# Decode attention with a 268 MB cache: p.v with the values moving in four column groups, keys folded in place, wo as four rows a lane

## The chip, the cores and the metric

The kernel runs on one core of one Trainium2 chip. The metric is the device time of one execution in microseconds; several runs are taken and their median is given. The profile comes from one profiled execution. Engines are named as the profile names them: PE is TensorE (PEld its weight loads), DVE VectorE, ACT ScalarE, POOL GpSimd, SP SyncE. Nearly all transfers are issued on SP's queue and are carried by the core's 16 DMA engines.

## The reference

The output is the input plus an attention block and a gated MLP block, both on the normalised input. There is one new token for each of four batch entries, and every one of the 32 heads has its own cache of 4096 keys and values of 128 bf16 numbers.

```python
# x: (4, 1, 640); k_cache, v_cache: (4, 32, 4096, 128); wq: (640, 4096); wo: (4096, 640)
q = (xn @ wq) as (4, 32, 1, 128)
scores = einsum('bhqd,bhkd->bhqk', q, k) * 128 ** -0.5
p = softmax(scores)
o = einsum('bhqk,bhkd->bhqd', p, v)
attention = o as (4, 1, 4096) @ wo
# gMLP: z = gelu(xn @ w_in); z1, z2 = halves of z (864 each); g = w_sp * layernorm(z2) + b_sp
result = x + attention + (z1 * g) @ w_out
```

Keys and values are 134 MB each and are read once. A key meets a single query, so the scores are a matrix times a vector for each pair of batch entry and head.

## The kernel before

**Tiles and slots.** Four heads of one batch entry make a tile: 128 partitions ("lanes"), 32 lanes a head, and in each lane 128 rows (NC) of 128 numbers, 4 MB. There are 32 tiles of keys and 32 of values (NT = 32; tile i belongs to head group i // 4 and batch entry i % 4). A pool of five slots (`kv`) holds them. The first three slots hold wq (two loads) and the gMLP's weights at the start. `load` (L115) fetches one tile in one transfer on SP; the last tile of values comes in four pieces, 64, 32, 16 and 16 rows of a lane (`V_CUTS`). `pump` (L137) issues loads in a fixed order, roughly v(i), k(i+2), as far as the tile that held the slot has been marked as used; the transfer itself waits on the engines that last touched the slot. At two places (`EXTRA_K`) two key tiles follow each other, so that at the end the keys are ahead and the last four tiles to come are values. `load_wo` (L148) fetches the 640 KB of wo that one head group needs, in the third of its four tiles; the last one comes as four pieces of 160 KB, behind everything else.

**Scores of a tile.** `stage_q` (L365) brings the query into every lane: four matmuls spread the four heads' queries over 32 lanes each (four groups of 32 columns of PE), and ACT copies the result to bf16. The scores come in four quarters: `product` (L381) multiplies a quarter of the keys with the query on DVE into a buffer `prod`; `fold_half` (L390) adds the upper 64 of the 128 products to the lower 64 into `folded`. After each half, `sums` (L402) lets PE add these 64 numbers down to 8: eight matmuls with the identity, each over 512 columns, into one PSUM bank. `row_sums` (L415) reduces the 8 to one on DVE. The second half's `row_sums` of a tile stands in the next tile's step.

**Softmax.** `lane_max` (L425) takes the largest score of each lane, `turn_max` (L430) turns these 128 numbers into one row by an fp32 transpose on PE, `head_max` (L435) takes the maximum of each head, `spread_max` (L446) spreads the negative scaled maxima over all lanes by an fp32 matmul, and `exps` (L453) computes the exponentials on ACT, head by head, with their sums per lane into `acc`. The weights go to `p_m`: for each of the 128 rows of a lane four columns, one a head, with zeros where a lane belongs to another head.

**p.v.** `weighted` (L469) makes the values the stationary operand: for each of the 128 rows of a lane it loads 128x128 values as weights and moves four columns of `p_m` through; the result, 128 numbers of the head dimension on partitions by head and batch entry, gathers in PSUM. After the fourth tile of a group, `group_den` (L485) sums `acc` over the lanes by an fp32 matmul with ones and inverts it on DVE, `group_norm` (L494) scales, and `group_proj` (L501) multiplies by wo into `out_ps`.

**Order.** The order on PE, DVE, ACT and SP is written out by hand in the loop at L536. The p.v of tile i - 1 (later i - 2 and i - 3) stands in step i, behind the first `sums`. Each step ends with marking the keys as used and with `pump`. Behind the loop (L571 to L591) come the last tile's softmax, the p.v of the last two tiles of values, the last projection and the output. At the start, q is projected by 160 matmuls with wq as the stationary operand (L216), and the gMLP runs ahead of the loop.

Of the kernel before, what the change touches and what calls it, by code (L numbers as in the profile page):

```python
# [16 lines left out]
EXTRA_K = (24, 28)  # L17


@with_exitstack  # L20
def kernel(
# [31 lines left out]
    NQ = 4  # L53
    QC = NC // NQ
# [7 lines left out]
    NOH = D // 2  # L62

    const = ctx.enter_context(tc.tile_pool(name="const", bufs=1))
    kv = ctx.enter_context(tc.tile_pool(name="kv", bufs=KV_SLOTS))
    wop = ctx.enter_context(tc.tile_pool(name="wop", bufs=1))
    prod = ctx.enter_context(tc.tile_pool(name="prod", bufs=1))
    fold = ctx.enter_context(tc.tile_pool(name="fold", bufs=2))
# [5 lines left out]
    ps_m = ctx.enter_context(tc.tile_pool(name="ps_m", bufs=2, space=PSUM))  # L74
# [4 lines left out]


# [64 lines left out]
    wo_v = A_wo.rearrange("(j h p) n -> j p h n", p=P, h=HT)  # L145
    wo_tiles = {}

    def load_wo(j):  # L148
        wo_tiles[j] = wop.tile([P, HT, D], BF16, name="wo")
        if j == HG - 1:  # L150
            for hh in range(HT):
                nc.sync.dma_start(out=wo_tiles[j][:, hh, :], in_=wo_v[j][:, hh, :])
            return
        nc.sync.dma_start(out=wo_tiles[j][:], in_=wo_v[j])
# [3 lines left out]


    ident = const.tile([P, P], BF16)  # L160
    make_identity(nc, ident[:])
    ident_f = const.tile([P, P], FP32)
    nc.vector.tensor_copy(out=ident_f[:], in_=ident[:])
# [4 lines left out]
    scale_row = const.tile([1, P], FP32)  # L168
    nc.vector.memset(scale_row[:], scale_qk)
# [4 lines left out]
    p_m = [const.tile([P, NC, HT], BF16, name=f"pm{b}") for b in range(Bsz)]  # L174
    acc = [const.tile([P, HT, Bsz], FP32, name=f"acc{g}") for g in range(NACC)]
    for t in p_m + acc:
        nc.gpsimd.memset(t[:], 0.0)


# [29 lines left out]
    xnT = const.tile([P, DC, Bsz], BF16)  # L209
    nc.vector.tensor_copy(out=xnT[:], in_=xnT_ps[:])  # L210

    q_ps = ps_m.tile([P, H, Bsz], FP32, tag="m", name="q_ps")
    for h in range(H):
        for c in range(DC):
            t, i = wq_parts[c]
            nc.tensor.matmul(  # L216
                out=q_ps[:, h, :],
                lhsT=t[:, i, h * Dh : (h + 1) * Dh],
                rhs=xnT[:, c, :],
                start=(c == 0),  # L220
                stop=(c == DC - 1),
            )
    qT = const.tile([P, H, Bsz], BF16)
    nc.vector.tensor_copy(out=qT[:], in_=q_ps[:])  # L224


# [15 lines left out]


# [10 lines left out]
    def gmlp():  # L254
        zz, gw, gt, gz, sq = (gm[n] for n in ("zz", "gw", "gt", "gz", "sq"))
        zT = ps_pv.tile([P, 2, NFC, Bsz], FP32, tag="pv", name="zT")
        for t in range(2):
            f1 = t * Fh + NFF * P
            w_t = w_in_sb[:, :, t * Fh : f1].rearrange("p c (f k) -> p c k f", k=NFF)
            for k in range(NFC):  # L260
                for c in range(DC):
                    nc.tensor.matmul(
                        out=zT[: P if k < NFF else FT, t, k, :],
                        lhsT=w_t[:, c, k, :] if k < NFF else w_in_sb[:, c, f1 : f1 + FT],
                        rhs=xnT[:, c, :],
                        start=(c == 0),
                        stop=(c == DC - 1),
                    )
# [94 lines left out]
    folds, sums_ps, maxes = {}, {}, {}  # L363

    def stage_q(i):  # L365
        hg, b = divmod(i, Bsz)
        qb_ps = ps_m.tile([P, Dh], FP32, tag="m", name="qbc_ps")
        for hh in range(HT):
            nc.tensor.matmul(  # L369
                out=qb_ps[hh * LN : (hh + 1) * LN, :],  # L370
                lhsT=qT[:, HT * hg + hh, b : b + 1].to_broadcast([P, LN]),
                rhs=ident[:],
                start=True,
                stop=True,
            )
        qbcs[i] = small.tile([P, Dh], BF16, name="qbc", bufs=3)
        nc.scalar.copy(out=qbcs[i][:], in_=qb_ps[:])  # L377

    prods = {}

    def product(i, q):  # L381
        t = prods[i, q] = prod.tile([P, QC, Dh], BF16, name="prod")
        nc.vector.tensor_tensor(  # L383
            out=t[:],
            in0=k_tiles[i][:, q * QC : (q + 1) * QC, :],
            in1=qbcs[i][:, None, :].to_broadcast([P, QC, Dh]),
# [3 lines left out]
    def fold_half(i, q):  # L390
        t = prods.pop((i, q))
        half, part = divmod(q, 2)
        if part == 0:
            folds[i, half] = fold.tile([P, HC, HD2], BF16, name="folded")
        nc.vector.tensor_tensor(  # L395
            out=folds[i, half][:, part * QC : (part + 1) * QC, :],
            in0=t[:, :, 0:HD2],
            in1=t[:, :, HD2:Dh],
            op=ALU.add,
        )  # L400

    def sums(i, half):  # L402
        t = folds.pop((i, half))
# [21 lines left out]
    def lane_max(i):  # L425
        m1 = small.tile([P, 1], FP32, name="m1")
        nc.vector.tensor_reduce(out=m1[:], in_=scores[i][:], axis=AX.X, op=ALU.max)  # L427
        maxes[i] = m1

    def turn_max(i):  # L430
        mT = ps_m.tile([1, P], FP32, tag="m", name="mT")
        nc.tensor.transpose(out=mT[:], in_=maxes[i][:], identity=ident_f[:])  # L432
        maxes[i] = mT

    def head_max(i):  # L435
        nm = small.tile([1, HT], FP32, name="nm")
        nc.vector.tensor_reduce(  # L437
            out=nm[:],
            in_=maxes[i][:].rearrange("a (h p) -> a h p", h=HT),
            axis=AX.X,  # L440
            op=ALU.max,
            negate=True,
        )
        maxes[i] = nm

    def spread_max(i):  # L446
        nb_ps = ps_m.tile([P, HT], FP32, tag="m", name="nb_ps")
        nc.tensor.matmul(  # L448
            out=nb_ps[:], lhsT=scale_row[:], rhs=maxes[i][:], start=True, stop=True
        )  # L450
        maxes[i] = nb_ps

    def exps(i):  # L453
        hg, b = divmod(i, Bsz)
        nb = small.tile([P, HT], FP32, name="nb")
        nc.scalar.copy(out=nb[:], in_=maxes.pop(i)[:])  # L456
        s_sb, pm, a = scores.pop(i), p_m[b], acc[hg % NACC]
        for hh in range(HT):
            ps = slice(hh * LN, (hh + 1) * LN)
            nc.scalar.activation(  # L460
                out=pm[ps, :, hh],
                in_=s_sb[ps, :],
                func=ACT.Exp,
                bias=nb[ps, hh : hh + 1],
# [4 lines left out]
    def weighted(i, c0=0, c1=NC):  # L469
        hg, b = divmod(i, Bsz)  # L470
        if b == 0 and c0 == 0:
            pvs[hg] = ps_pv.tile([P, HT, Bsz], FP32, tag="pv", name="pv")
        v_nat, pm = v_tiles[i], p_m[b]
        for c in range(c0, c1):
            nc.tensor.matmul(  # L475
                out=pvs[hg][:, :, b],
                lhsT=v_nat[:, c, :],
                rhs=pm[:, c, :],
                start=(c == 0),
                stop=(c == NC - 1),  # L480
            )

    gr = {}

    def group_den(hg):  # L485
        den = ps_m.tile([P, HT, Bsz], FP32, tag="m", name="den")
        nc.tensor.matmul(  # L487
            out=den[:], lhsT=ones_sq[:], rhs=acc[hg % NACC][:], start=True, stop=True
        )
        rden = small.tile([P, HT, Bsz], FP32, name="rden")  # L490
# [3 lines left out]
    def group_norm(hg):  # L494
        o_n = small.tile([P, HT, Bsz], BF16, name="o_n")
        nc.vector.tensor_tensor(
            out=o_n[:], in0=pvs.pop(hg)[:], in1=gr[hg][:], op=ALU.mult
        )
        gr[hg] = o_n
# [20 lines left out]

    turns = {}
# [8 lines left out]
    with tc.manual_schedule(engines={E.PE, E.DVE, E.Activation, E.SP}):  # L530
# [5 lines left out]
        for i in range(NT):  # L536
            j = turns.get(i)
            product(i, 0)
            fold_half(i, 0)
            at(i - 1, row_sums, 1)  # L540
            at(i - 1, lane_max)
            at(i - 1, turn_max)
            group(turns.get(i - 1, -1), group_proj)
            product(i, 1)
            at(i - 1, head_max)
            at(i - 1, spread_max)
            at(i - 1, exps)
            fold_half(i, 1)
            sums(i, 0)
            product(i, 2)  # L550
            if i + 2 < NT:
                stage_q(i + 2)
            fold_half(i, 2)
# [3 lines left out]
            for jj in due:  # L557
                weighted(jj)
                group(jj, group_den)
# [62 lines left out]
```

## Time and profile before

| what | value |
|---|---|
| median of three runs | 673.95 us (673.77 to 673.96) |
| span of the profiled execution, first to last instruction | 671.3 us |
| runs' median over that span (what lies around it) | 2.65 us |
| mean granted TensorE clock | 0.627 |
| busy: DVE, PE, ACT | 507.1, 392.5, 94.4 us |
| bytes moved, mean rate | 282.98 MB, 422 GB/s |

The page does not give the profiled execution's own time, only its span; the difference to the median of the runs is taken as what lies around it. The span is cut into 40 slices for the rows of busy tenths, where 9 stands for 90% or more. A group row gives a line of the kernel, the engine, the operation, output and inputs, shapes and count; then busy time, mean duration in ns, and the idle time in front with what ended it. A row of the windows view gives start and end, the length, busy time and number of instructions on PE, PEld, DVE, ACT and POOL, and at the end the granted clock, the mean busy share of the 16 DMA engines and GB/s. In a DMA queue row stand packets, MB and the time of the packets as a share of 16 engines' span; the queue called "instruction" brings the programs of the engines.

### The profile page before, as it was taken

To read this page: it belongs to the slowest core of one execution; us is meant where nothing else is said; L and a number is where in the kernel's file an instruction comes from. 1 tells how busy PE (TensorE), PEld (TensorE's weight loads), DVE (VectorE), ACT (ScalarE), POOL (GpSimd) and SP (SyncE) were. 2 spreads that over 40 slices of the span, in tenths; PEclk is the share of its full clock that TensorE was granted. 3 is DMA by queue.
4 is the path that set the end of the run, shared out by engine and by line. 5 is a ranking of instruction groups with operands and counts; after the bars stand their busy time and mean duration, and the time that the engine had idled before them with its cause. 6 is when DMAs were issued, how large, how long until landed. Compare 5 with 4: busy or idle time off the path is not lost.

```text
span 671.3 us, 11493 instructions
## 1 busy us (share of the span) xinstructions
PE 392.5 (58%) x5193; PEld 213.8 (32%) x5193; DVE 507.1 (76%) x433; ACT 94.4 (14%) x329; POOL 2.7 (0%) x13
## 2 busy tenths in 40 slices
PE   1627765546656456574556755456655557556576
PEld 1503333233333233342233333133333224233154
DVE  1299896966779777787777788676786999876961
ACT  0202111101111101111101111101111111101111
POOL 1000000000000000000000000000000000000000
PEclk9999675666656556666575556566666655656566
DMA  9999999999999999999999999999999999999995
GB/s 371 418 437 436 429 426 428 429 425 432 430 426 431 431 427 431 427 428 430 431 431 421 433 430 427 429 425 429 430 436 423 429 435 430 418 432 429 433 418 203
DMA packets 14684, 282.98 MB, mean 422 GB/s; under 512 B 1344, under 2 KB 5548, under 8 KB 5932
## 3 DMA queue, kind: packets, MB, share of 16 engines
q1 hardware_dynamic: 14616, 282.25, 98.5%
q8 instruction: 40, 0.66, 0.4%
q14 instruction: 8, 0.07, 0.0%
q10 hardware_dynamic: 20, 0.01, 0.0%
HBM read 282.24 MB, written 0.01 MB: 420 GB/s over the span
## 4 chain that ended last, share of the span: by engine, by line
DMA 55%; DVE 27%; PE 16%; issue 1%; SPq 0%; DVEq 0%
DMA k_nat<-in_A_k_cache_dram 50%; DVE prod L383 15%; PE s_ps L407 8%; DVE folded L395 8%; PE pv L475 7%; DMA v_nat<-in_A_v_cache_dram 6%; DVE s_sb L418 3%; DVE m L427 1%; DVE nm L437 0%; PE den L487 0%; PE qbc_ps L369 0%; DVE rden L491 0%; PE out_ps L505 0%; SPq L100 0%; SPq L89 0%
## 5 line engine op out<-in xcount | busy, mean ns | idle before, releaser
L383 DVE TENSOR_TENSOR prod<-k_nat,qbc 128x4096 bf16<-128x4096 bf16 x128 | 292.7, 2287 | 82.8 <-DMA k_nat<-in_A_k_cache_dram 81.2
L407 PE MATMUL s_ps<-folded,ident 128*128 128x512 bf16 x512 | 225.5, 619 | 80.8 <-DVE folded L395 80.4
L395 DVE TENSOR_TENSOR folded<-prod 128x2048 bf16<-128x2048 bf16 x128 | 156.1, 1220 | 3.3
L407 PEld LDWEIGHTS <-ident 128*128 128x128 bf16 x512 | 71.1, 139 | 190.7 <-issue 189.9
L475 PE MATMUL pv<-pm,v_nat 128*128 128x4 bf16 x4096 | 111.3, 167 | 3.5 <-issue 3.0
L475 PEld LDWEIGHTS <-v_nat 128*128 128x128 bf16 x4096 | 108.9, 100 | 7.1 <-issue 3.7
L432 PE MATMUL mT<-ident_f,m 128*1 128x128 f32 x32 | 11.2, 350 | 111.7 <-DVE m L427 111.7
L460 ACT ACTIVATE pm<-s_sb,nb 32x128 bf16<-32x128 f32 x128 | 74.0, 578 | 2.6
L456 ACT COPY nb<-nb_ps 128x4 f32<-128x4 f32 x32 | 5.2, 162 | 475.8 <-PE nb_ps L448 475.8
L448 PE MATMUL nb_ps<-nm,scale_row 1*128 1x4 f32 x64 | 17.7, 345 | 59.0 <-DVE nm L437 59.0
L418 DVE TENSOR_REDUCE s_sb<-s_ps 128x64 f32<-128x512 f32 x64 | 43.6, 682 | 9.6 <-PE s_ps L407 6.5
L432 PEld LDWEIGHTS mT<-ident_f,m 128*1 128x1 f32 x32 | 2.5, 79 | 138.5 <-DVE m L427 102.3
L448 PEld LDWEIGHTS nb_ps<-nm,scale_row 1*128 1x128 f32 x64 | 15.6, 302 | 68.6 <-issue 57.2
L460 ACT ACTIVATION_READ_ACCUMULATOR pm<-s_sb,nb 32x1 f32 x128 | 32.2, 251 | 0.0
L491 DVE RECIPROCAL rden<-den 128x16 f32<-128x16 f32 x8 | 2.1, 258 | 32.6 <-PE den L487 32.6
L377 ACT CAST qbc<-qbc_ps 128x128 bf16<-128x128 f32 x32 | 8.4, 266 | 78.5 <-PE qbc_ps L369 78.4
L369 PEld LDWEIGHTS <-qT 128*32 128x32 bf16 x128 | 3.4, 99 | 24.3 <-issue 23.8
L224 DVE CAST qT<-q_ps 128x128 bf16<-128x128 f32 x1 | 0.3, 291 | 14.3 <-PE q_ps L216 14.3
L216 PE MATMUL q_ps<-xnT,wq 128*128 128x4 bf16 x160 | 4.6, 167 | 9.5 <-DMA wq<-in_A_wq_dram 9.5
L427 DVE TENSOR_REDUCE m<-s_sb 128x1 f32<-128x128 f32 x32 | 9.2, 286 | 1.1
L437 DVE TENSOR_REDUCE nm<-mT 1x4 f32<-1x128 f32 x32 | 8.7, 272 | 0.5 <-PE mT L432 0.5
L369 PE MATMUL qbc_ps<-ident,qT 128*32 128x128 bf16 x128 | 8.8, 272 | 0.4 <-DVE qT L224 0.4
(69 smaller groups left out, 54.1 us busy)
## 6 DMA issues: line engine op xcount, KB each, us to landing
k_nat<-in_A_k_cache_dram SPq DMA_DIRECT2D x32, 4096.0 KB, 43.6
v_nat<-in_A_v_cache_dram SPq DMA_DIRECT2D x31, 4096.0 KB, 35.6
wo<-in_A_wo_dram SPq DMA_DIRECT2D x7, 640.0 KB, 44.5
wq<-in_A_wq_dram SPq DMA_DIRECT2D x1, 4096.0 KB, 12.2
w_sb<-in_B_w_in_dram SPq DMA_DIRECT2D x1, 2160.0 KB, 19.0
v_nat<-in_A_v_cache_dram SPq DMA_DIRECT2D x1, 2048.0 KB
wq<-in_A_wq_dram SPq DMA_DIRECT2D x1, 1024.0 KB, 14.2
v_nat<-in_A_v_cache_dram SPq DMA_DIRECT2D x1, 1024.0 KB
```

Of the source, the lines that this page charges most:

```text
L369: nc.tensor.matmul(out=qb_ps[hh * LN : (hh + 1) * LN, :], lhsT=qT[:, HT * hg + hh, b : b + 1].to_broadcast([P, LN]), rhs=ident[:], start=True,
L377: nc.scalar.copy(out=qbcs[i][:], in_=qb_ps[:])
L383: nc.vector.tensor_tensor(out=t[:], in0=k_tiles[i][:, q * QC : (q + 1) * QC, :], in1=qbcs[i][:, None, :].to_broadcast([P, QC, Dh]), op=ALU ...
L395: nc.vector.tensor_tensor(out=folds[i, half][:, part * QC : (part + 1) * QC, :], in0=t[:, :, 0:HD2], in1=t[:, :, HD2:Dh], op=ALU.add,)
L407: nc.tensor.matmul(out=s[:], lhsT=ident[:], rhs=t[:, :, g * RW : (g + 1) * RW], start=(g == 0), stop=(g == n - 1),)
L418: nc.vector.tensor_reduce(out=scores[i][:, half * HC : (half + 1) * HC], in_=sums_ps.pop((i, half))[:], axis=AX.X, op=ALU.add,)
L427: nc.vector.tensor_reduce(out=m1[:], in_=scores[i][:], axis=AX.X, op=ALU.max)
L432: nc.tensor.transpose(out=mT[:], in_=maxes[i][:], identity=ident_f[:])
L437: nc.vector.tensor_reduce(out=nm[:], in_=maxes[i][:].rearrange("a (h p) -> a h p", h=HT), axis=AX.X, op=ALU.max, negate=True,)
L448: nc.tensor.matmul(out=nb_ps[:], lhsT=scale_row[:], rhs=maxes[i][:], start=True, stop=True)
L460: nc.scalar.activation(out=pm[ps, :, hh], in_=s_sb[ps, :], func=ACT.Exp, bias=nb[ps, hh : hh + 1], scale=scale_qk, accum_out=a[ps, hh, b : ...
L475: nc.tensor.matmul(out=pvs[hg][:, :, b], lhsT=v_nat[:, c, :], rhs=pm[:, c, :], start=(c == 0), stop=(c == NC - 1),)
```

## The change

The change rewrites several steps.

- The projection of q swaps its operands: the normalised input, widened from 4 to 32 columns, is the stationary operand, and wq moves through in pieces of 512 columns, four groups of 32 PE columns side by side. The rows that come out (`q_rows`) are spread over the lanes by one matmul a tile with one column of the identity (`stage_q`), and ACT copies the four heads' parts in four copies.
- The keys are multiplied in place, half a tile at a call, and folded in place. `prod` and `folded` are gone, and PE's `sums` read the key slot itself, with 128 numbers from row to row instead of 64.
- The maximum over the lanes of a head is taken on DVE by a transpose in blocks of 32x32 and a second reduce. The fp32 transpose and the spreading matmul on PE are gone.
- p.v swaps its operands too: 32 columns of `p_m` (two batch entries x four rows of a lane x four heads, half of them zero) are the stationary operand and 512 values of a lane move through. 32 such matmuls a tile go round four column groups, two tiles gather in one PSUM bank, and each row is multiplied with the values of all four positions. ACT copies the bank to SBUF (`take`), and `group_pick` selects the matching blocks by eight fp32 matmuls with a mask (`pick`). `group_turn` scales by the denominators and transposes in blocks of 32x32, which leaves the head dimension as p = 4 rows a lane; wo is therefore loaded as four consecutive rows a lane (5120 bytes in a run where 1280 were).
- The last group ends in its own way: the first half of the last tile goes by the column groups and the selection, the rest by 64 matmuls with the values stationary as before, and wo comes by head as before.
- wo has two buffers, the small PSUM pool three banks instead of two.

The diff, cut to its core:

```diff
+    wop = ctx.enter_context(tc.tile_pool(name="wop", bufs=WO_BUFS))
...
-        nc.sync.dma_start(out=wo_tiles[j][:], in_=wo_v[j])
+        nc.sync.dma_start(out=wo_tiles[j][:], in_=rows.rearrange("(p j) n -> p j n", j=HT))
...
+                nc.tensor.matmul(
+                    out=q_ps[g * QD : (g + 1) * QD, :],
+                    lhsT=xnT[:, c, :],
+                    rhs=t[:, i, hg * GW : (hg + 1) * GW],
+                    start=(c == 0),
+                    stop=(c == DC - 1),
+                )
...
+        for hh in range(HT):
+            ps = slice(hh * LN, (hh + 1) * LN)
+            nc.scalar.copy(out=qbcs[i][ps, :], in_=qb_ps[ps, hh, :])
+
+    def product(i, half):
         nc.vector.tensor_tensor(
+            out=half_of(i, half),
+            in0=half_of(i, half),
+            in1=qbcs[i][:, None, :].to_broadcast([P, HC, Dh]),
             op=ALU.mult,
         )
...
+            out=t[:, :, 0:HD2], in0=t[:, :, 0:HD2], in1=t[:, :, HD2:Dh], op=ALU.add
...
+    def head_max(i):
         m1 = small.tile([P, 1], FP32, name="m1")
         nc.vector.tensor_reduce(out=m1[:], in_=scores[i][:], axis=AX.X, op=ALU.max)
+        mt = small.tile([P, LN], FP32, name="mt")
+        nc.vector.transpose(out=mt[:], in_=m1[:].to_broadcast([P, LN]))
+        nm = small.tile([P, 1], FP32, name="nm")
+        nc.vector.tensor_reduce(out=nm[:], in_=mt[:], axis=AX.X, op=ALU.max, negate=True)
...
+        for g in range(ng):
+            cg = g % CB
             nc.tensor.matmul(
+                out=pvs[hg, a][cg * QD : (cg + 1) * QD, :],
+                lhsT=pm[:, g, :],
+                rhs=v_nat[:, g * CB : (g + 1) * CB, :],
+                start=(t == 0 and g < CB),
+                stop=(t == 1 and g >= ng - CB),
             )
...
+    def take(hg, a):
+        o = taken[hg, a] = small.tile([P, CB, Dh], FP32, name="o_rows")
+        nc.scalar.copy(out=o[:].rearrange("p c d -> p (c d)"), in_=pvs.pop((hg, a))[:])
...
+    def group_pick(hg):
+        o_ps = ps_m.tile([P, Dh], FP32, tag="m", name="o_ps")
+        for a in range(2):
+            o = taken.pop((hg, a))
+            for c in range(CB):
+                nc.tensor.matmul(
+                    out=o_ps[:],
+                    lhsT=pick[:, a, c, :, :].rearrange("p h q -> p (h q)"),
+                    rhs=o[:, c, :],
...
             product(i, 0)
+            at(i - 1, row_sums, 1)
+            at(i - 1, head_max)
+            group(last, group_pick)
             fold_half(i, 0)
+            at(i - 1, exps)
             sums(i, 0)
+            group(last, group_turn)
             if i + 2 < NT:
                 stage_q(i + 2)
+            product(i, 1)
...
+                consume(jj)
             row_sums(i, 0)
+            fold_half(i, 1)
             sums(i, 1)
+            group(last, group_proj)
...
+        weighted(NT - 1, V_CUTS[1])
+        take(hg, 1)
+        o_ps = ps_m.tile([P, HT, Bsz], FP32, tag="m", name="o_last")
...
+        for c in range(V_CUTS[1], NC):
+            nc.tensor.matmul(
+                out=o_ps[:, :, b],
+                lhsT=v_tiles[NT - 1][:, c, :],
+                rhs=pm[:, c // CB, b % 2, c % CB, :],
```

More of the change, by code (lines that the diff above doesn't have):

```diff
@@ L362 @@
     qbcs, scores, pvs = {}, {}, {}
[L363 removed]
+    sums_ps, maxes = {}, {}
     def stage_q(i):
         hg, b = divmod(i, Bsz)
[L367 to L377 removed]
```

242 lines of the change are left out of this document (128 added, 114 removed).

## The prediction

> **What bounds the kernel now.** I read the page first: busy times, the slices of the span with the DMA share, the DMA queues, the costliest groups.
>
> ```profile
> span 671.3 us, 11493 instructions
> PE 392.5 (58%) x5193; PEld 213.8 (32%) x5193; DVE 507.1 (76%) x433; ACT 94.4 (14%) x329; POOL 2.7 (0%) x13
> DMA  9999999999999999999999999999999999999995
> q1 hardware_dynamic: 14616, 282.25, 98.5%
> q8 instruction: 40, 0.66, 0.4%
> L383 DVE TENSOR_TENSOR prod<-k_nat,qbc 128x4096 bf16<-128x4096 bf16 x128 | 292.7, 2287 | 82.8 <-DMA k_nat<-in_A_k_cache_dram 81.2
> L407 PE MATMUL s_ps<-folded,ident 128*128 128x512 bf16 x512 | 225.5, 619 | 80.8 <-DVE folded L395 80.4
> L395 DVE TENSOR_TENSOR folded<-prod 128x2048 bf16<-128x2048 bf16 x128 | 156.1, 1220 | 3.3
> L475 PE MATMUL pv<-pm,v_nat 128*128 128x4 bf16 x4096 | 111.3, 167 | 3.5 <-issue 3.0
> L418 DVE TENSOR_REDUCE s_sb<-s_ps 128x64 f32<-128x512 f32 x64 | 43.6, 682 | 9.6 <-PE s_ps L407 6.5
> L427 DVE TENSOR_REDUCE m<-s_sb 128x1 f32<-128x128 f32 x32 | 9.2, 286 | 1.1
> ```
>
> The sixteen DMA engines are full in 39 of 40 slices. DVE, the busiest engine, has 507 us of work and waits 81 us for keys. So the stream of 282 MB sets the pace; a change to PE, DVE or ACT counts only where it moves the stream's end, or what comes after it. Then the windows: a stretch of the middle, and the end of the stream.
>
> ```profile
> 200.00:300.00 100.00, 60.47 (x775) 32.08 (x775) 81.96 (x66) 13.73 (x50) 0.00 (x0) 0.57 1.01 429
> 654.00:658.00 4.00, 2.34 (x21) 1.10 (x20) 1.26 (x3) 0.19 (x2) 0.00 (x0) 0.90 0.95 387
> 658.80:666.60 7.80, 5.90 (x207) 5.82 (x205) 0.26 (x1) 1.52 (x6) 0.00 (x0) 0.50 0.55 214
> 666.60:669.00 2.40, 1.74 (x28) 0.77 (x24) 0.49 (x2) 0.35 (x1) 0.00 (x0) 0.50 0.01 5
> ```
>
> The last three numbers are granted clock, DMA share, GB/s. At 429 GB/s a 4 MB tile takes 9.8 us, so a pair of tiles (one step of the loop) 19.6 us. The third row matters most: for 7.8 us only about half of the engines move data (0.55). Every transfer is spread over all sixteen, so eight are done some 7.4 us before the other eight (0.55 of 7.8 us is 8 engines for 7.8 us and little more), and a tile has landed only when the slowest has brought its part. Something had been delaying half of the engines. My candidate is the queue of PE's instructions: 40 packets, 0.4% of 16 x 671.3 us, which is 43 us of a single engine's time; shared by eight, 5.4 us each. That is the size of the lag, though not all of it.
>
> After the stream comes a short chain (the chain of waits, in order of time).
>
> ```profile
> 661.86 1.90 issue
> 663.75 3.38 PE pv L475 x120
> 667.15 0.18 DVE o_n L496
> 667.38 1.27 PE out_ps L505 x5
> 668.68 0.48 DVE res L589
> ```
>
> The projection starts at 667.38, just after DMA falls silent. About 4 us follow, which the change keeps.
>
> **The change part by part.**
>
> *PE's program.* Before, 2 x 5193 instructions filled 40 packets, 260 each. p.v is 128 pairs of weight load and matmul a tile before, 32 after; the projection of q 160 before, 40 after; the fp32 turns of the maximum go. The changed program has about 3970 PE instructions, an fp32 matmul counted as four: 15 packets. If eight engines take them in turn, each gets two, not five: 3/5 of 7.4 us, 4.4 us off the stream's end. Lower bound: if sixteen share them, 25/40 of 43 us over 16 is 1.7 us. Upper bound: 25/40 of 7.4, 4.6. I take **4.4**, because a half share at the end is what delays on eight engines look like, and delays on sixteen do not.
>
> *wo as four rows a lane.* Seven loads of 640 KB go from 512 rows of 1280 bytes to 128 runs of 5120 bytes. The windows around three of their landings, and a neighbour without one:
>
> ```profile
> 120.00:130.00 10.00, 4.56 (x19) 1.68 (x18) 9.89 (x10) 0.00 (x0) 0.00 (x0) 0.67 1.03 428
> 200.00:210.00 10.00, 4.48 (x17) 1.36 (x16) 9.87 (x9) 0.00 (x0) 0.00 (x0) 0.62 1.05 433
> 270.00:280.00 10.00, 7.93 (x144) 5.27 (x145) 6.04 (x8) 2.75 (x10) 0.00 (x0) 0.67 0.98 417
> 280.00:290.00 10.00, 4.21 (x17) 1.33 (x16) 9.89 (x9) 0.00 (x0) 0.00 (x0) 0.67 1.03 430
> ```
>
> No dip shows; the spread, 417 to 433, would hide 0.3 us in 10. So a load gains between 0 and 0.3 us, seven 0 to 2.1; I take the middle, **1.0**. The last load stays in rows of 1280 bytes.
>
> The Trainium skill ("DMA: Bandwidth & Descriptors", Why small descriptors are slow) gives a packet three cycles beside its 32-byte beats. By that rule 43 cycles for 40 beats become 163 for 160, an estimate of 0.6 us over the seven loads, and the time would be 0.4 us above mine. The rows, with their noise, allow both.
>
> *DVE.* Slope and fixed cost come from product and fold: 1067 ns for 2048 more elements, so 153 ns a call. A product of 8192 is then 4.42 us, a fold of 4096 2.29: 13.4 us a tile where 4 x 2.287 + 4 x 1.220 = 14.0 stood. Two row sums (1.36), the lane maximum, a 32-wide transpose and a 32-wide maximum (each at most the 0.29 us of a 128-wide reduce) make 15.6 us a tile. Hidden under 19.6 us of DMA, with 4 us to spare. In-place output is not seen at this size; it decides nothing until a product costs 2 us more (6.4). Every fourth tile the reciprocal still waits for the denominator behind p.v, as it does now (total, times, longest):
>
> ```profile
> DVE rden L491 <- PE den L487: 32.6, 8, 4.5
> ```
>
> That is some 4 us, just within the pair's 19.6.
>
> *The key slot is held longer.* It is read last by PE's row sums, no longer by DVE's product.
>
> ```profile
> 617.03 2.30 DVE prod L383
> 631.67 1.75 SPq L120 DMA_DIRECT2D v_nat<-in_A_v_cache_dram  x4
> DMA to landing us min/median/max: 29.5/35.4/44.8
> 513.10 3.57 PE L407 MATMUL s_ps<-folded,ident 128*128 128x512 bf16 x8 [0.48 <-DVE folded L395]
> ```
>
> Before, SP issued the next load 14.6 us into the tile; now after 15.4 us of DVE and 3.6 of eight matmuls, 19.0: 4.4 us later. Behind it on SP stand the next key load and wo. Cover: of at least 29.5 us to landing 9.8 are the load's own transfer, so about 20 us of other transfers lie ahead. Cost nothing; without cover, up to 4.4 us a step.
>
> *p.v in four column groups, PE's load.* The nearest row is the old staging of q, four column groups of 128 columns.
>
> ```profile
> 516.60 0.30 PE L369 MATMUL qbc_ps<-ident,qT 128*32 128x128 bf16 x4
> 661.05 0.50 PEld L487 LDWEIGHTS den<-acc,ones_sq 128*128 128x128 f32 x2
> 657.36 0.29 PEld L448 LDWEIGHTS nb_ps<-nm,scale_row 1*128 1x128 f32 x2 [0.65 <-issue]
> ```
>
> A 512-column matmul of the sums takes 3.57/8 = 0.45 us, so 128 columns 0.11; four in a row would need 0.45, yet they fit into 0.30. So groups run beside each other. 32 matmuls of 512 columns in fours are 3.6 us, what 128 old pairs took (3.38 for 120). With 16 for the sums and one for q, PE has 11.2 us a pair of tiles: hidden. Bounds per matmul: 0.11 us (full overlap) to 0.45 (none). The extra selection (eight fp32 matmuls, under 1 us each) falls once in four tiles, where PE idles.
>
> *The start.* q's projection becomes 40 such matmuls: 18 us if nothing overlaps.
>
> ```profile
> 13.02 0.27 PE L216 MATMUL q_ps<-xnT,wq 128*128 128x4 bf16 x4 [7.34 <-DMA wq<-in_A_wq_dram]
> 34.63 2.31 DVE prod L383
> ```
>
> From 13.0 that is 31 us at worst, and the first product stands at 34.6 behind its keys. The gMLP could then run some 10 us into it; the 20 us of queued transfers and DVE's 4 us a pair cover that.
>
> *ACT.*
>
> ```profile
> L377 ACT CAST qbc<-qbc_ps 128x128 bf16<-128x128 f32 x32 | 8.4, 266 | 78.5 <-PE qbc_ps L369 78.4
> 668.65 0.41 ACT L588 CAST res<-out_ps 4x320 bf16<-4x320 f32 x1 [8.30 <-PE out_ps L505]
> ```
>
> Staging q becomes four copies (at most 0.27 us each, the old one's time), and 16 copies of p.v come in (0.56 us of 512 elements, by the line through 0.27 at 128 and 0.41 at 320): some 35 us on 94, hidden except the last.
>
> *After the stream's end E.* The issues at the end:
>
> ```profile
> v_nat<-in_A_v_cache_dram SPq DMA_DIRECT2D x1, 1024.0 KB
> v_nat<-in_A_v_cache_dram SPq DMA_DIRECT2D x2, 512.0 KB, 32.7
> wo<-in_A_wo_dram SPq DMA_DIRECT2D x4, 160.0 KB, 16.2
> ```
>
> Behind the last tile's first half come 2.7 MB, 6.4 us, so it lands at E - 6.4. Half clock: its 16 matmuls end at E - 4.4; eight fp32 selections at 0.50 us (their two weight loads, first row of L487) end near E - 0.4, the copy from PSUM beside the first four; 64 matmuls on the rest at 28 ns (3.38 us for 120) end at E + 1.4. Before, they ended at about E, so +1.4. Full clock: 0.29 us a selection (L448 at clock 1.00), all is done when wo lands, so 0. I take **+0.9**, nearer the half clock that the window at the end shows (0.50).
>
> The Trainium skill ("TensorE: Matmul & The Clock Gate", Part 1: The HAM clock gate) says that PE falls to half rate after an idle window of some 3.4 us. By that rule the end runs at half clock and the time is 0.5 us above mine; the trace agrees as far as 0.50 stands in that row, yet 0.90 just before it.
>
> **Sum.** -4.4 - 1.0 + 0.9 = -4.5 us on a span of 671.3: 666.8. The median of the runs is 673.95, 2.65 us above the span; the same lies around it after: **669.4 us**.
>
> **The rivals.**
>
> *The lag is not the instructions'.* If eight engines are slow by themselves, or sixteen share the instruction packets, only 1.7 us go wo brings nothing and the end still grows by 0.9: 673.1, no change. For it: the row gives 5.4 of 7.4 us at most. Against it: what else would spare eight engines. 14%.
>
> *The column groups do not run beside each other (slower).* At the clock of the middle window (0.57) a matmul is 0.22/0.57 = 0.39 us. The loop just hides that (49 x 0.39 = 19.1 us of 19.6), but at the end 48 of them stand between the last tiles and the output: 18.7 us instead of 5.4, so -4.5 + 13.3 = +8.8: 682.8. It decides from about 0.21 us a matmul (48 x 0.21 is 4.5 us above 5.4). Against it: 0.30 us for four above. 10%.
>
> The Trainium skill ("TensorE: Matmul & The Clock Gate", Part 3: Packing small matmuls) measured 2.38 times for three column tiles, not three; by that 32 matmuls take an estimated 4.5 us and the end 0.5 us more, well short of this rival.
>
> *In place is slow on DVE, or the late slot starves the stream.* From 6.4 us a product, DVE becomes the bound, each 0.1 us above it costing 6.4 us over 64 products; at 6.8 the time is near 695. Nothing in the trace speaks for it. 6%.
>
> **How the numbers follow.** The forecast has 70%. A measurement tells about 0.2% (1.35 us) from no change. Faster 0.70, same 0.14 (the first rival), slower 0.16 (the other two). The forecast's own range: all gains at their largest with no growth, 673.95 - 4.6 - 2.1 = 667.2, to 673.95 - 3.4 + 1.4 = 672.0 (1.0 us less from the instructions or from wo). The range takes in the first rival up to its worst end (-1.7 + 1.4): **667.2 to 673.6**, which leaves 16% out.
>
> **What would show it.** Right: q8 with 14 to 17 packets; the stretch of half share shorter than 4 us; DMA at nine tenths in all slices but the last; p.v in about 3.6 us a tile; product near 4.4 us. Wrong: a half share still above 6 us (the lag has another cause); DVE's wait for keys near zero or DMA slices under nine tenths (DVE or the slots bound); more than 6 us between the end of DMA and the end of the span (the selection weighs more).

## The result, and the profile after

The changed kernel takes **668.1 us** (median of four runs, 666.8 to 668.35) against 673.96 (673.77 to 674.04) for the kernel before, run beside it: a ratio of 0.9911, with a 95% interval of 0.9897 to 0.9925, so 5.9 us faster. The forecast was 669.4 in a range of 667.2 to 673.6, and a span of 666.8; the profiled execution has 666.6.

Rows of the page of the changed kernel, which answer to the first fence of the prediction:

```profile
span 666.6 us, 5047 instructions
PE 304.9 (46%) x1985; PEld 125.7 (19%) x1985; DVE 499.6 (75%) x350; ACT 127.2 (19%) x441; POOL 4.7 (1%) x15
DMA  9999999999999999999999999999999999999996
q1 hardware_dynamic: 11928, 282.25, 98.9%
q8 instruction: 15, 0.25, 0.1%
L400 DVE TENSOR_TENSOR k_nat<-k_nat,qbc 128x8192 bf16<-128x8192 bf16 x64 | 282.7, 4418 | 106.3 <-DMA k_nat<-in_A_k_cache_dram 106.0
L409 DVE TENSOR_TENSOR k_nat<-k_nat 128x4096 bf16<-128x4096 bf16 x64 | 146.0, 2281 | 0.0
L471 PE MATMUL pv<-v_nat,pm 128*32 128x512 bf16 x1008 | 72.9, 441 | 6.5 <-DMA v_nat<-in_A_v_cache_dram 6.5
L483 ACT COPY o_rows<-pv 128x512 f32<-128x512 f32 x16 | 9.4, 586 | 30.3 <-PE pv L471 30.3
```

The stream still bounds the kernel: nines in 39 slices, and DVE waits longer for keys (106 us, 81.2 before). PE's program (q8) has gone from 40 packets to 15. The windows view of a stretch in the middle and of the stream's end:

```profile
200.00:300.00 100.00, 47.34 (x303) 19.40 (x302) 77.43 (x51) 18.56 (x67) 0.00 (x0) 0.76 1.01 431
...
658.00:659.00 1.00, 1.00 (x6) 1.00 (x7) 0.00 (x0) 0.00 (x0) 0.00 (x0) 0.50 0.76 294
659.00:660.00 1.00, 1.00 (x6) 1.00 (x6) 0.00 (x0) 0.00 (x0) 0.00 (x0) 0.50 0.64 239
660.00:661.00 1.00, 1.00 (x22) 1.00 (x22) 0.00 (x0) 0.00 (x0) 0.00 (x0) 0.50 0.57 196
661.00:662.00 1.00, 1.00 (x44) 1.00 (x41) 0.00 (x0) 0.00 (x0) 0.00 (x0) 0.50 0.12 40
```

In the middle the rate is what it was (431 GB/s, 429 before). The gain is at the end: the stretch with part of the engines idle lasts from 658 to about 661.2, 3.2 us instead of 7.8. After that PE is longer in the way than before. The chain of waits (start, length, what):

```profile
655.27 1.90 PE pv L471 x16
657.17 3.53 PE o_last L616 x16
660.70 1.70 PE o_last L625 x64
662.40 0.02 issue
662.43 0.19 DVE o_n_last L633
662.61 0.04 issue
662.66 1.27 PE out_ps L531 x8
```

DMA is all but silent from about 661.2 on, but the 64 matmuls of p.v end only at 662.4, 1.2 us later; in the kernel before, p.v ended at 667.13, 0.5 us after the 666.6 at which its half share ends. The selections (L616) took 3.53 us at a clock of 0.50. This is the "+0.9" of the prediction.

### The profile page after: what moved, and what is told of

It is laid out like the page before. It is cut to its first block, busy times and chain, and to the rows that moved or that the text cites. A ratio compares the mean times of both kernels' runs of the same rounds, so it can differ in the third digit from the quotient of the medians.

```text
span 666.6 us, 5047 instructions
## 1 busy us (share of the span) xinstructions
PE 304.9 (46%) x1985; PEld 125.7 (19%) x1985; DVE 499.6 (75%) x350; ACT 127.2 (19%) x441; POOL 4.7 (1%) x15
## 4 chain that ended last, share of the span: by engine, by line
DMA 68%; DVE 23%; PE 7%; issue 2%; DVEq 0%
DMA k_nat<-in_A_k_cache_dram 62%; DVE k_nat L400 12%; DVE k_nat L409 7%; PE s_ps L418 4%; DMA v_nat<-in_A_v_cache_dram 4%; DVE s_sb L429 2%; DMA wq<-in_A_wq_dram 2%; PE pv L471 1%; PE q_ps L217 1%; PE o_last L616 1%; DVE m L438 0%; DVE mt L440 0%; DVE o_n L514 0%; DVE nm L442 0%; PE o_last L625 0%
## 5 line engine op out<-in xcount | busy, mean ns | idle before, releaser
L400 DVE TENSOR_TENSOR k_nat<-k_nat,qbc 128x8192 bf16<-128x8192 bf16 x64 | 282.7, 4418 | 106.3 <-DMA k_nat<-in_A_k_cache_dram 106.0
L418 PE MATMUL s_ps<-k_nat,ident 128*128 128x512 bf16 x512 | 181.1, 518 | 331.9 <-DVE k_nat L409 331.8
L409 DVE TENSOR_TENSOR k_nat<-k_nat 128x4096 bf16<-128x4096 bf16 x64 | 146.0, 2281 | 0.0
L471 PE MATMUL pv<-v_nat,pm 128*32 128x512 bf16 x1008 | 72.9, 441 | 6.5 <-DMA v_nat<-in_A_v_cache_dram 6.5
L394 ACT CAST qbc<-qbc_ps 32x128 bf16<-32x128 f32 x128 | 32.9, 257 | 135.1 <-PE qbc_ps L384 134.0
L471 PEld LDWEIGHTS <-pm 128*32 128x32 bf16 x1008 | 26.9, 109 | 59.1 <-issue 44.5
L384 PE MATMUL qbc_ps<-q_rows,ident 128*128 128x512 bf16 x32 | 18.0, 568 | 0.0
L503 PEld LDWEIGHTS o_ps<-o_rows,pick 128*128 128x128 f32 x112 | 15.9, 218 | 1.4 <-issue 0.6
L503 PE MATMUL o_ps<-o_rows,pick 128*128 128x128 f32 x112 | 15.6, 300 | 0.0
L483 ACT COPY o_rows<-pv 128x512 f32<-128x512 f32 x16 | 9.4, 586 | 30.3 <-PE pv L471 30.3
```

Source lines behind the costliest of these rows:

```text
L384: nc.tensor.matmul(out=qb_ps[:], lhsT=ident[:, row : row + 1].to_broadcast([P, P]), rhs=q_rows[r][:], start=True, stop=True,)
L394: nc.scalar.copy(out=qbcs[i][ps, :], in_=qb_ps[ps, hh, :])
L400: nc.vector.tensor_tensor(out=half_of(i, half), in0=half_of(i, half), in1=qbcs[i][:, None, :].to_broadcast([P, HC, Dh]), op=ALU.mult,)
L409: nc.vector.tensor_tensor(out=t[:, :, 0:HD2], in0=t[:, :, 0:HD2], in1=t[:, :, HD2:Dh], op=ALU.add)
L418: nc.tensor.matmul(out=s[:], lhsT=ident[:], rhs=t[:, :, g * RW : (g + 1) * RW], start=(g == 0), stop=(g == n - 1),)
L471: nc.tensor.matmul(out=pvs[hg, a][cg * QD : (cg + 1) * QD, :], lhsT=pm[:, g, :], rhs=v_nat[:, g * CB : (g + 1) * CB, :], start=(t == 0 and ...
```

## The experiments

The theory: the stream of DMA sets the time; the packets of PE's program delay its end, some engines more than others; wo's longer runs shorten it a little; the new end loses about 1 us to PE at half clock; DVE, ACT and p.v in the loop are hidden. The rivals: PE's work rather than its program; wo alone; column groups that do not overlap; a cost of DVE's in-place output.

### The program made long again

After each step's p.v the changed kernel gets 100 short spare matmuls (the identity times four columns of it).

```diff
...
+            idle_pairs(100)
             row_sums(i, 0)
```

> The changed kernel, with 100 spare pairs of weight load and matmul a step on PE (the identity, four columns, into a spare PSUM tile that nothing reads). PE's program grows from some 3970 to some 10370 instructions, as many as before the change; PE's time grows by about 2.8 us a step, which 19.6 us of DMA cover. Theory (each packet of PE's program delays one of eight DMA engines): 40 packets of the instruction queue again, five for each of eight engines, the stretch of half share at the end back to 6 to 8 us, and the time 4.4 us over the changed kernel's 668.1: about 672.5. Rival (the lag is not the instructions'): half share as short as in the changed kernel, 668.1.

It took 672.82 us (671.71 to 673.53), a ratio to the kernel before of 0.9984 (0.9976 to 0.9993). From the page, and from the windows of its end:

```profile
q8 instruction: 40, 0.66, 0.4%
```

```profile
658.00:665.90 7.90, 5.95 (x66) 4.78 (x66) 0.00 (x0) 0.58 (x1) 0.00 (x0) 0.64 0.54 210
```

With 40 packets again, the half share is back for 7.9 us (0.54; 0.55 for 7.8 us in the kernel before), and 4.7 of the 5.9 us gained are gone. The theory holds so far: 4.7 us over 25 packets, 0.19 us each. (The spares also bring PE 91 us more work; a later kernel tells the two apart.)

### Longer still

The same with 150 spares a step.

```diff
...
+            idle_pairs(150)
```

> The changed kernel with 150 spare pairs a step instead of 100, so 52 or 53 packets of PE's program. Theory (each packet beyond 15 costs the end of the stream the same, 4.7 us over 25 packets, 0.19 us each): 15 + 37.5 packets, 668.1 + 7.1 = 675.2, slower than the kernel before although only the program is longer; the stretch of half share is 10 us or longer. Rival (the cost stops growing once the end is late): 672 to 673.5.

```profile
q8 instruction: 53, 0.87, 0.5%
```

674.80 us (674.29 to 676.49), a ratio of 1.0021 (1.0012 to 1.003): slower than the kernel before, by nothing but the spares. Over the changed kernel it is 6.7 us for 38 packets, 0.18 each; the cost goes on growing. In the profiled execution the last selections ran at full clock (1.96 us), which by the experiments below is worth about 1 us, so at equal clock a packet costs nearer 0.2. One detail missed: the stretch of reduced share was not 10 us, as the windows show.

```profile
659.00:667.60 8.60, 6.35 (x114) 4.38 (x106) 1.25 (x5) 3.03 (x10) 0.00 (x0) 0.90 0.54 211
```

### PE's work without its program

Ten spare matmuls of 512 columns a step (the identity times rows of q): much work in few instructions.

```diff
...
+            long_spares(10)
             row_sums(i, 0)
```

> The changed kernel, with 10 spare matmuls of 512 columns a step on PE (results unread): PE's time grows by 2 to 4 us a step, as much as or more than with the 100 short pairs, but its program by only 640 instructions, two or three packets. Theory (what delays the DMA engines is the program, not PE's work): 668.1 to 669.0. Rival (PE's busy time or its reads of SBUF slow the transfers): 672 or more, as with the short pairs.

```profile
PE 357.8 (54%) x2273; PEld 148.9 (22%) x2305; DVE 499.5 (75%) x350; ACT 127.2 (19%) x441; POOL 4.7 (1%) x15
...
q8 instruction: 18, 0.29, 0.2%
```

668.0 us (667.98 to 669.28), ratio 0.9918 (0.9903 to 0.9933): the changed kernel's time, with 53 us more on PE. So it is the program and not the work, in the main. The comparison is not perfectly clean: three packets more should cost 0.6 us, and its end ran at a higher clock (0.93 from 657.8 to 661.4), which by the experiments below is worth about 1. That leaves some 0.4 us that the work may have cost, and, for the 91 us of the short spares, up to 0.7 of their 4.7.

### The kernel before with a quarter of p.v

```diff
-        for c in range(c0, c1):
+        step = 4 if i < NT - 2 else 1
+        for c in range(c0, c1, step):
...
```

> The kernel before, with p.v over every fourth of the 128 rows of a lane in the first 30 tiles (three quarters of those products are left out), the last two tiles as they were. PE's program falls from 10386 to some 4630 instructions, 18 packets; nothing else in the kernel is touched, and the end is the same. Theory: the slowest engines get two or three packets instead of five, the stretch of half share shrinks to 3 to 4.5 us, and 3.0 to 4.4 us go: 669.6 to 671.0. Rival (the gain came from the selection of other steps of the change, such as wo or DVE): 673.7 to 674.0.

Measured: 668.94 (668.75 to 669.19), ratio 0.993 (0.9916 to 0.9944). Its q8 row and two windows of its end:

```profile
q8 instruction: 18, 0.29, 0.2%
```

```profile
659.00:660.00 1.00, 0.13 (x5) 0.14 (x6) 0.00 (x0) 0.00 (x0) 0.00 (x0) 0.50 0.85 328
...
659.00:662.30 3.30, 1.60 (x48) 1.43 (x48) 0.00 (x0) 0.00 (x0) 0.00 (x0) 0.50 0.68 255
```

The kernel before gains 4.8 us from 22 packets fewer (673.76 to 668.94, both from one chip), and its lag shrinks to 3.3 us, the changed kernel's. The time is below the 669.6 to 671.0 expected: 0.22 us a packet. Both directions, a longer program in the new kernel and a shorter one in the old, give nearly the same price.

### wo alone

```diff
-        nc.sync.dma_start(out=wo_tiles[j][:], in_=wo_v[j])
+        rows = A_wo[j * HT * P : (j + 1) * HT * P]
+        nc.sync.dma_start(out=wo_tiles[j][:], in_=rows.rearrange("(p j) n -> p j n", j=HT))
```

> The kernel before, with the first seven loads of wo as four consecutive rows a lane (5120 bytes in a run, not 1280); the projection then multiplies with rows in another order than its other operand has. Forecast's term: 1.0 us less, within 0 and 2.1: 673.0. Rival: a run of 1280 bytes moves as fast as one of 5120, 674.0.

In the kernel before this gives 672.32 us (671.74 to 672.58), ratio 0.998 (0.9971 to 0.9989): 1.4 us faster, 0.7 to 2.0 by the interval. The end lags as before (windows view):

```profile
658.00:666.00 8.00, 6.07 (x215) 5.99 (x212) 0.26 (x1) 1.53 (x6) 0.00 (x0) 0.51 0.47 181
```

So wo's part and the program's part are separate. The packet records of the changed kernel's trace give a like price: a row of 1280 bytes takes 55 ns (median) and a run of 5120 bytes 200, where four rows make 220; over 896 runs and 16 engines that is some 1.1 us. (In this kernel wo's rows meet the head dimension in another order than in the reference; the work is the same.)

### In place alone

The kernel before, with product and fold written over the keys, still in quarters.

```diff
-        t = prods[i, q] = prod.tile([P, QC, Dh], BF16, name="prod")
+        t = prods[i, q] = k_tiles[i][:, q * QC : (q + 1) * QC, :]
...
+            out=t,
+            in0=t,
...
-            out=folds[i, half][:, part * QC : (part + 1) * QC, :],
+            out=t[:, :, 0:HD2],
```

> The kernel before, with the product and the fold in place in the key slot, still in quarters; everything else as before. The slot is now held until PE's sums have read it. Theory (DVE writes in place at the same rate, and about 20 us of queued transfers cover the later release): product 2.29 us, fold 1.22 us, DMA at nine tenths in all slices but the last, 673.8. Rival (in place is slower, or the late release starves the stream): 680 or more.

```profile
L383 DVE TENSOR_TENSOR k_nat<-k_nat,qbc 128x4096 bf16<-128x4096 bf16 x128 | 291.9, 2280 | 82.2 <-DMA k_nat<-in_A_k_cache_dram 82.2
```

673.82 us (673.26 to 674.42), ratio 1.0 (0.9991 to 1.001). A product in place takes 2280 ns where it took 2287, and the slot that is held longer costs nothing.

### The end: other work, or a warmer PE

Two ways to take the selection at half clock off the path. First, the last tile goes wholly with the values stationary, as in the kernel before, so that the selections come before its values:

```diff
...
-        weighted(NT - 1, V_CUTS[1])
         take(hg, 1)
...
-        for c in range(V_CUTS[1], NC):
+        for c in range(NC):
```

> The changed kernel, with the whole last tile of values by 128 matmuls with the values stationary; the selection of the tile in front of it then runs before the last tile lands. Theory (the selection at half clock stands between the last landing and the projection): the projection starts when the last piece of wo lands, the 1.1 us between the end of DMA and the end of p.v go, 667.0. Rival (the end of DMA alone sets the time, or PE's 48 further pairs and their program's packets take the place of the selection): 668.1 or more.

Second, the changed kernel as it is, with spare matmuls (the identity times 512 columns of keys) around the last p.v but one:

```diff
...
+        keep_warm(24)
         weighted(NT - 2)
+        keep_warm(12)
```

> The changed kernel, with 24 spare matmuls of 512 columns on PE ahead of the p.v of the last tile but one and 12 behind it, results unread, so that PE does not idle while it waits for the last tiles. Theory (PE's clock falls to half in the idle stretch before the end, and the selection at the end runs at half clock): granted clock near 1.00 in the last 15 us, the eight selections take 2.3 us instead of 3.5, and 1.0 to 1.5 us go: 666.6 to 667.1. Rival (the selection's weight loads cost the same at any clock, or the wait for the last tile's half lets the clock fall again): 668.1.

Both took 666.99 us (666.84 to 667.18, ratio 0.9902, 0.9888 to 0.9915; and 666.72 to 667.3, ratio 0.9899, 0.9884 to 0.9913). The chain of the first, and PE's timeline of the second:

```profile
632.39 27.81 DMA v_nat<-in_A_v_cache_dram
660.20 0.05 issue
660.25 0.60 PE o_last L624 x16
```

```profile
655.02 1.05 PE L471 MATMUL pv<-v_nat,pm 128*32 128x512 bf16 x16
656.00 1.96 PE L625 MATMUL o_last<-pick,o_rows 128*128 128x16 f32 x16
657.80 1.55 PE L634 MATMUL o_last<-pm,v_nat 128*128 128x4 bf16 x48
660.08 0.56 PE L634 MATMUL o_last<-pm,v_nat 128*128 128x4 bf16 x16 [0.72 <-DMA v_nat<-in_A_v_cache_dram]
```

The last 16 matmuls now wait for the last values to land. At full clock the selections take 1.96 us, not 3.60, and p.v of half a tile 1.05, not 1.90. So the changed kernel's end costs 1.1 us by the medians (668.1 - 666.99), and 1.5 to 1.7 by the profiled spans (666.6 against 665.1 and 664.9). The intervals of the ratios overlap, so the case rests on the traces. The second kernel shows that the clock is the cause, since its work at the end is the changed kernel's and more.

### Eight matmuls of p.v in one column group in a row

```diff
-            cg = g % CB
+            cg = g * CB // ng
...
```

> The changed kernel, with the 32 matmuls of p.v going through the four column groups one group after the other (eight in a row on each) instead of round and round; the same matmuls, the same result. Theory (the groups run beside each other only when neighbours use different ones): p.v of a tile takes 7 us (full clock) to 14 us (half clock) instead of 3.6, the loop hides most of it, and at the end 48 such matmuls stand before the selection: 3 to 14 us more, 671 to 682. Rival (four groups bring nothing, PE streams one matmul after the other in any case): p.v as long as in the changed kernel, 668.1.

This missed: 666.77 us (666.57 to 666.91), ratio 0.9894 (0.9878 to 0.9911), among the fastest of all. The group of p.v on the page and the end on PE's timeline:

```profile
L472 PE MATMUL pv<-v_nat,pm 128*32 128x512 bf16 x1008 | 150.8, 393 | 4.9 <-DMA v_nat<-in_A_v_cache_dram 2.6
```

```profile
650.40 4.53 PE L472 MATMUL pv<-v_nat,pm 128*32 128x512 bf16 x32 [1.46 <-DMA v_nat<-in_A_v_cache_dram]
654.86 0.40 PE L605 MATMUL den_all<-acc,ones_sq 128*128 128x16 f32 x2
655.22 1.08 PE L472 MATMUL pv<-v_nat,pm 128*32 128x512 bf16 x16
656.23 1.96 PE L617 MATMUL o_last<-pick,o_rows 128*128 128x16 f32 x16
```

Two things went against the expectation. The order took away only part of the overlap: p.v is busy 150.8 us, twice the 72.9, yet 4.53 us a tile at full clock is 0.14 us a matmul; and the last half tile, whose runs are of four, takes 1.08 us, as fast as one by one (1.05 above). And the longer p.v keeps PE so busy that the clock stays at 1.00 until 659, past the selections: what the loop hides costs nothing, and the end gains the 1.1 us. So this was no test of the second rival, and two more kernels were made.

### Four in a row, and all in one group

Four in a row:

```diff
-            cg = g % CB
+            cg = g // CB % CB
...
```

> The changed kernel with the matmuls of p.v going through the column groups four in a row instead of one by one or eight by eight. Theory (a matmul of another group starts beside the running ones as long as it stands only a few places behind in the program): p.v takes 1.9 to 2.3 us a tile at full clock, as one by one, PE is no busier than in the changed kernel, the last selections run at half clock (3.5 us), and the time is 667.8 to 668.4. Rival (whatever does not alternate loses the overlap): 4.5 us a tile as with eight in a row, the clock stays at 1.00 to the end, and the time is 666.6 to 667.0.

The group's row says 73.5 us for p.v, so nothing of the overlap is lost.

```profile
L472 PE MATMUL pv<-v_nat,pm 128*32 128x512 bf16 x1008 | 73.5, 438 | 7.3 <-DMA v_nat<-in_A_v_cache_dram 5.3
```

The time is on neither side alone: the profiled execution took 668.31 us with its selections at half clock (3.53 us in its chain, as in the changed kernel), the three others 666.7 to 666.78; median 666.76, ratio 0.99 (0.9885 to 0.9915). The changed kernel does the same the other way round: three runs at 668.1 to 668.35, one at 666.8. Since the profiled executions on the 668 side both end at half clock and the kernels with a full clock lie at 666.8 to 667.0, I read the two levels as the two clocks at the end; the runs on the 666.8 side have no trace, so this is argued. Their mean granted clocks are on record and settle it only in part: four in a row has 0.723 in the run at 668.31 and 0.735 to 0.742 in the others, but the changed kernel 0.734, 0.726 and 0.723 at 668.1 to 668.35 and 0.735 at 666.8. In the clock records of all traces the clock is 0.50 or 1.00 and changes only on a grid of 3.41 us, so it may depend on where the grid lies whether the same wait of 5.8 us lowers it; no run shows that.

All in one group but the first four of each two tiles:

```diff
-            cg = g % CB
+            cg = g if t == 0 and g < CB else 0
...
```

> The changed kernel with nearly all matmuls of p.v in one column group (of two tiles' 64 only the first four are spread); the sums over the groups, and so the output, are the same. Theory: without any overlap a matmul of 512 columns takes 0.22 us at full clock (the sums' spacing there), 7.0 us a tile, hidden in the loop, and PE is then so busy that the clock stays at 1.00. At the end the 32 and 16 matmuls of the last tiles, the selections (1.96 us) and the 64 matmuls (1.5 to 2.1 us) run one behind the other from 650.4 on, the projection starts near 665 instead of 661.1, and the time is 669 to 672. The prediction's second rival at its own price (0.39 us a matmul): 682.8, and DVE's wait for the denominators doubled. If overlap brings nothing that reaches the end: 666.8 as with eight in a row.

It took 674.99 us (674.05 to 676.07), ratio 1.0019 (1.0009 to 1.0029), slower than the kernel before, and above the 669 to 672 expected. Its group and its chain:

```profile
L471 PE MATMUL pv<-v_nat,pm 128*32 128x512 bf16 x1008 | 221.4, 395 | 2.1 <-issue 1.8
```

```profile
640.59 13.55 PE pv L471 x64
654.14 1.83 PE s_ps L418 x8
655.97 6.36 PE pv L471 x32
662.33 0.33 PE den_all L604 x2
662.66 3.56 PE pv L471 x16
666.22 1.89 PE o_last L616 x16
668.11 1.60 PE o_last L625 x64
```

Without overlap a matmul takes 0.20 to 0.22 us at full clock, 6.36 us a tile. My expectation started p.v of the last tile but one at 650.4, when its values land; but two tiles' p.v (13.55 us) still stood in front of it, and it started at 655.97. So the overlap decides the sign of the change, as the rival had it. Only its price was not that of the rival: the clock is 1.00 in all windows from 650 to 670, so 0.21 us a matmul where the rival took 0.39.

## Why the prediction was right, point by point

**The stream bounds, and the lag at its end is the program's.** Right. Forecast -4.4 us for 25 packets; measured 4.7 by making the program long again, and 4.8 for 22 packets in the kernel before. The step that carried it, from a half share to eight delayed engines with five packets each, foretold that 3/5 of the lag would go; it went from 7.8 to 3.2 us. The 14% rival (the lag has another cause, or sixteen engines share the packets) is excluded by the two directions and by the size.

The traces bear the eight out. In the kernel before the share is 0.52 from 662 to 664, 8.3 engines of 16, and in the packet records the lengths of the instruction packets repeat with a period of eight (before: 1107, 1099, 1086, 1018, 1018, 1073, 1068, 1061 ns, then 1107, 1108, 1086, 1018, 1026, 1073, 1069, 1068), as if eight engines took them in turn; no record names the engine. The size was in part luck. The packets' own time was 5.4 of the 7.4 us, so by it alone 3.2 us would have gone; the prediction scaled the whole lag, and the runs bear that out, but what the rest of a packet's cost is stays open.

**wo.** Right in sign, the term mis-sized: -1.0 taken, -1.4 measured, inside its 0 to 2.1. By the rule of the Trainium skill ("DMA: Bandwidth & Descriptors", Why small descriptors are slow) it would have been an estimated 0.6; the measured interval, 0.7 to 2.0, lies just above, so a short packet seems to cost more here than three cycles. That 1.0 came near was the middle of a wide range, not a reading.

**DVE, in place, and the slot.** Right: a product 4.42 us, a fold 2.28, and in the kernel before no time from being in place. The landings of the key loads show the cover still there: one lands at the soonest 30.4 us after its issue, of which 9.8 are its own transfer. (The 29.5 us of the prediction are those of the value loads, pieces of a tile among them; a key load took 31.3 or more before.)

```profile
DMA to landing us min/median/max: 30.4/41.3/42.7
```

**p.v and ACT.** Right: hidden. The staging of q and the copies of p.v bring ACT from 94.4 to 127.2 us, 33 for the 35 forecast. The start is hidden too: the 40 matmuls of q's projection take 4.55 us, and the first product stands at 34.73 us, where it stood at 34.63. p.v takes 3.60 us a tile at half clock, the forecast's figure, and 1.91 at full clock (two rows of PE's timeline):

```profile
513.02 1.91 PE L471 MATMUL pv<-v_nat,pm 128*32 128x512 bf16 x32
...
650.46 3.60 PE L471 MATMUL pv<-v_nat,pm 128*32 128x512 bf16 x32 [5.79 <-DMA v_nat<-in_A_v_cache_dram]
```

Against 6.36 us in one group, the four groups are worth 3.3 times at full clock. In the Trainium skill ("TensorE: Matmul & The Clock Gate", Part 3: Packing small matmuls) three column tiles are worth 2.38; the price of a row of four staged queries, 0.30 us, was the better guide.

**The end.** Forecast +0.9, between 1.4 at half clock and 0 at full; measured 1.1 by the medians, 1.5 by the spans at the two clocks. So the mechanism was right, and 0.9 itself a compromise between two values of which an execution has one or the other. (A slip in the sum: 16 matmuls at its 0.11 us end at E - 4.6, not E - 4.4, which makes +1.2 at half clock.) The row above shows why it ran at half clock: PE had waited 5.79 us for values before it, and 0.50 stands in every window from 650 on; with 1.46 us of waiting (eight in a row) it stayed at 1.00. The rule of the Trainium skill that I had weighed ("TensorE: Matmul & The Clock Gate", Part 1: The HAM clock gate), half rate after an idle window of some 3.4 us, agrees with both. It does not cover every row: with the 100 short spares PE had waited only 2.40 us, and the selections still took 3.60 us, at half clock.

**What lies around the span.** Wrong, by 0.9 us, which is most of the forecast's 1.3 us error. I took 2.65 us, the runs' median less the span of one profiled execution. In the changed kernel the profiled execution took 668.35 us with a span of 666.6, 1.75 us around it, and an execution of the kernel before beside the later experiments 673.7 with a span of 671.9, 1.8. So the profiled execution of before, with 671.3, had taken some 673.1, and was 0.85 us faster than the median. Against its own span the sum was right to 0.2 us (666.8 for 666.6). That also leaves a remainder: the parts as measured, -4.7 - 1.4 + 1.1 = -5.0, come near the 4.7 us between the two profiled spans, but leave 0.9 of the 5.9 us between the medians. The kernel before simply spreads: its 53 executions beside the later experiments have spans from 671.1 to 672.7, with 1.74 to 1.85 us around them, and the profiled one was among the shortest. Why it spreads, the runs do not tell.

**The rivals.** The second one (10%) was right that lost overlap would reach the end and turn the sign: from 0.21 us a matmul, it said, and one group with 0.20 to 0.22 came out 1.1 us slower than the kernel before. That its threshold fits so well is partly luck: it counted 48 matmuls at the end, where 112 stood one behind the other from 640.59 on. It did not happen because the groups do overlap. The third (6%) did not happen either: the product takes 4.42 us, and in place alone costs nothing.

## What to carry to other kernels

In a kernel that is bound by its stream of DMA, a long program of an engine is part of the stream too: count its packets, some 260 instructions each here, before looking at what the instructions do, and look at the stream's last microseconds for a share of about a half. PE, made faster in the loop, can be slower at the end, because its waits lower its clock: look at the granted clock of the last 10 us, and put there either work that does not wait, or less work. And when a forecast goes from a span to a time, take both from the same execution.

## What the runs showed of the hardware

A packet of PE's program costs this kernel 0.18 to 0.22 us, some five times what its 16 KB take at the stream's 430 GB/s (0.04 us). The Trainium skill ("Runtime: NRT & Kernel Launch", Instruction fetch mechanics) has the refill in blocks of 16 KiB, which agrees with 0.66 MB in 40 packets, and calls its cost mostly hidden, which does not hold for the stream here. For PE it may not always hold either: in the kernel before, PE stood still inside its p.v for 1.12 us at 648.48 and 1.90 us at 661.86 ("issue" in its chain), and the packet records have an instruction packet on its way from 647.2 to 648.2 and from 661.2 to 662.3; that PE waited for its program there is read from these times alone. Four column groups overlap alike whether the matmuls alternate or come four in a row (at half clock 3.60 and 3.64 us a tile); at full clock eight in a row lose more than half of the gain (4.53 us a tile for 1.91) and one group all of it (6.36). And spare work on PE made the end faster, by the clock alone: with 36 matmuls that compute nothing the median was 1.1 us lower, a level that one of the changed kernel's own four runs reached as well.
